# One-core attention with two expert layers: weights decoded by integer rounding, a third of the early decoding kept, and attention's order and engines from one table

## The chip, the cores and the metric

The kernel runs on one core of a Trainium2 chip. The metric is the device time of one execution in microseconds (us). Engines are named as in the profile: PE is the matrix engine and PEld its weight loads, DVE the vector engine, ACT the scalar engine, POOL the general engine, and SP the engine whose queue issues the DMA transfers.

## What is computed

Three steps follow one another, on 4 batches, 8 heads, 576 positions and 64 channels:

```python
scores = q @ k.T / sqrt(64);  scores[above diagonal] = -1e9
local  = softmax(scores) @ v
p      = where(q > 0, q + 1, exp(q))
mem    = (p @ M_prev) / (p @ z_prev + 1e-6)
x      = g * mem + (1 - g) * local            # g = sigmoid(beta), one per head
x      = x as [2304 tokens, 512]
x      = (silu(x @ w_gate) * (x @ w_val)) @ w_out        # inner width 1536
h      = x @ w_in                                        # inner width 2048
x      = where(h >= 1, h, where(h <= -1, 0, (h + 1)**2 / 4)) @ w_out2
```

All five weight arrays arrive as 64-bit floats, and the kernel itself turns them into 32-bit ones.

## The kernel before

**Numbers and products.** A 64-bit weight is two 32-bit words. `number` (L874 to L943) makes a 32-bit float of them: ACT takes the upper word without its sign (L892), DVE clamps it (L897), shifts it by the exponent's difference (L900) and puts the sign back (L903); a power of two cut from the result, times the lower word, is then added (L922). `split` (L953, L955) cuts a number into two rounded parts, hi and lo, and every product of the expert layers is a sum of three matmuls, hi by hi, lo by hi and hi by lo. The same is done with x: L831 and L834 in attention, `halves` (L1298 hi on ACT, L1301 lo on DVE) in the expert layers, which are called the MLP below.

**Attention** (0 to 254.8 us) goes over 16 pairs of heads. L644 and L678 make the scores, L658 masks them and takes the row maximum, L665 the exponential, L733 scales the rows (POOL; the last pair on DVE), L747, L749, L770 and L787 transpose, and L812 (`MZ`, the memory, times `P`) with L819 (values times `R`) make `av`, with the two heads in the two column halves of PE. `MZ` is padded with zeros to 128 rows. x goes to DRAM (`xs`, L848), already split. A planner (`Plan`) simulates the engines and puts the tasks of attention in order by a table of priorities (`ORDER`, `EARLY`, `COPY`) and each task has a fixed engine. A change of a matmul's form costs in it, and tasks of one form are kept together (`STAY`).

**Early work.** In attention's gaps POOL, DVE and ACT decode the first six of twelve blocks of `w_gate` and `w_val` (a block is 128 of the inner 1536 columns), and PE multiplies them with the x that is already there: L1170, 144 matmuls of 512 columns and 48 of 256. The results are put aside (`gv`, L1180).

**The MLP** has 2304 tokens in 6 groups of 384, two to a pair of groups. A second plan orders it by due times counted back from the end (`late_starts`):

- 254.8 to 366.4 us: `plain` (L1357), the rest of the first six blocks, 12 matmuls for one block and group;
- 366.4 to 496.4 us: `chain` (L1406), blocks 6 to 11, two blocks by two groups at a time in seven products instead of eight (`sums` and `x_pieces`, L1314 and L1335, form the sums of x that these need, `Weights.pair` those of the weights);
- 496.4 to 647.8 us: `down` (L1484), times `w_out`; 647.8 to 821.5: `w_in` in chains (L1406); 821.5 to 1018.5: `down2` (L1538).

x returns from `xs` by L1279, the early results by L1377, and the inner values are stored by L1368 and loaded again in `down`. SP issues all of these in the order of the plan; a load that waits holds up those behind it.

Of the kernel before, what the change touches and what calls it, by code (L numbers as in the profile page):

```python
# [11 lines left out]
U32 = mybir.dt.uint32  # L12
AF = mybir.ActivationFunctionType
# [5 lines left out]
P = 128  # L19
# [7 lines left out]
D0 = 6  # L27

FIRST_PAIRS = 3
STAY, TURN = 1.0e9, 165  # L30
# [3 lines left out]
EARLY = (-31758.7233, 79570.0368, -56626.7479, 43732.2004, 50493.6538, -22848.8291, 79748.7834, -38414.5005, 72019.3742, 35464.8591, 50747.3145, 30443.7461)  # L34
XH, GVO = 4, 3
X1, XS = 8, 25
RAW, WA, WH, TP, SU = 3, 5, 2, 7, 4
GROUP_AT, X_AT = (-58356.8242, -57686.563, -55609.5288), (21938.2824, -38157.4904, 79878.1715)
# [5 lines left out]
GV = (768, 512, 512)  # L44
# [1639 lines left out]
```

## Time and profile before

| what | us |
| --- | --- |
| median of three runs (1022.22 to 1025.65) | 1022.69 |
| the profiled execution | 1024.29 |
| its span | 1022.5 |
| PE busy in it | 1005.3 (98%) |
| DVE busy | 711.5 (70%) |
| ACT busy | 577.8 (57%) |
| POOL busy, all of it in attention | 214.5 (21%) |

The profiled execution has 1.8 us around its span and lies 1.6 us above the median. PE's shares are near the full span, so what counts is how much matmul work there is, in each stage, and where PE waits. The mean granted clock was 0.997.

### The profile page before, as it was taken

The numbers are of one execution on the slowest core, as the hardware profiler recorded it, in microseconds if no ns is written. First come the engines' busy times: TensorE is split into PE (matmuls) and PEld (weight loads), VectorE is DVE, ScalarE is ACT, GpSimd is POOL, SyncE is SP. The second block draws the span as 40 slices with busy tenths as digits, with TensorE's granted clock in tenths as the row PEclk, the third lists the DMA queues.
The fourth block names the chain that finished last, engine by engine and source line by source line (L and its number), as shares of the span: only waits on it lengthen the run. The fifth ranks groups of instructions, "written<-read, shape, count | busy, mean of one in ns | idle before, by whom it ended". The sixth has DMA issues, their size and how long they took to land.

```text
span 1022.5 us, 16609 instructions
## 1 busy us (share of the span) xinstructions
PE 1005.3 (98%) x5892; PEld 908.2 (89%) x5892; DVE 711.5 (70%) x1490; ACT 577.8 (57%) x1249; POOL 214.5 (21%) x300
## 2 busy tenths in 40 slices
PE   6999999999999999999999999999999999999998
PEld 5677777777999999999999999999999988888886
DVE  4887888885588777788778788876765346455451
ACT  5887898875333364636254444555444557567560
POOL 7899889893000000000000000000000000000000
PEclk8999999999999999999999999999999999999999
DMA  7787654327983542343976556255444596324420
GB/s 167 176 209 215 165 166 140 113 72 240 349 302 119 185 160 98 140 155 122 386 309 232 201 176 211 88 183 212 157 150 150 204 377 225 120 77 145 133 99 31
DMA packets 144547, 183.03 MB, mean 179 GB/s; under 512 B 70288, under 2 KB 101520, under 8 KB 144464
## 3 DMA queue, kind: packets, MB, share of 16 engines
q1 hardware_dynamic: 142366, 178.52, 52.9%
q0 software_dynamic: 768, 3.15, 0.9%
q8 instruction: 47, 0.77, 0.3%
q10 hardware_dynamic: 1330, 0.30, 0.1%
q14 instruction: 36, 0.29, 0.1%
HBM read 116.40 MB, written 65.54 MB: 178 GB/s over the span
## 4 chain that ended last, share of the span: by engine, by line
PE 93%; DMA 2%; POOL 2%; ACT 1%; DVE 1%; issue 0%; SPq 0%; ACTq 0%; DVEq 0%; POOLq 0%
PE mm L1406 30%; PE mm L1538 19%; PE mm L1484 13%; PE mm L1357 11%; PE av L819 4%; PE mm L1170 4%; PE s L644 3%; PE t L770 2%; PE av L812 2%; PE s L678 1%; POOL a L733 1%; DMA hs<-h 1%; PE t L787 1%; DMA xw<-park 1%; PE tp L598 1%; PE tq L540 1%
## 5 line engine op out<-in xcount | busy, mean ns | idle before, releaser
L1406 PE MATMUL mm<-xw 128*128 128x384 f32 x1512 | 269.5, 334 | 0.0
L1406 PEld LDWEIGHTS mm<-xw 128*128 128x128 f32 x1512 | 262.8, 188 | 0.1
L1538 PE MATMUL mm<-xw 128*128 128x512 f32 x864 | 196.2, 390 | 0.0
L1538 PEld LDWEIGHTS mm<-xw 128*128 128x128 f32 x864 | 162.2, 188 | 33.6
L1484 PE MATMUL mm<-xw 128*128 128x384 f32 x864 | 150.4, 335 | 0.3 <-DMA xw<-park 0.3
L1484 PEld LDWEIGHTS mm<-xw 128*128 128x128 f32 x864 | 149.8, 188 | 0.7 <-DMA xw<-park 0.7
L1357 PE MATMUL mm<-xw 128*128 128x384 f32 (+1 forms) x672 | 111.6, 327 | 0.0
L1357 PEld LDWEIGHTS mm<-xw 128*128 128x128 f32 x672 | 111.3, 188 | 0.2 <-DVE x L834 0.2
L733 POOL TENSOR_SCALAR a<-a,r,OGP 128x256 f32<-128x256 f32 (+4 forms) x135 | 90.7, 683 | 5.2 <-ACT a L665 3.4
L665 ACT ACTIVATE a<-a,mn 128x256 f32<-128x256 f32 (+3 forms) x128 | 71.0, 565 | 9.7 <-DVE mn L658 9.5
L1527 DVE SCALAR_TENSOR_TENSOR t<-r,t 128x768 f32<-128x768 f32 x48 | 46.0, 958 | 38.1 <-ACT t L1526 36.6
L1301 DVE TENSOR_TENSOR xw<-t,xw 128x768 fp32r<-128x768 f32 x48 | 45.9, 957 | 36.9 <-ACT xw L1298 36.9
L1298 ACT CAST xw<-t 128x768 fp32r<-128x768 f32 x48 | 40.1, 835 | 40.6 <-DVE t L1527 40.6
L658 DVE CUSTOM_DVE_ANT_0 a<-s,mask 128x512 f32<-128x512 f32 (+3 forms) x128 | 55.1, 485 | 5.8 <-PE s L644 5.5
L1428 ACT COPY mm<-mm 128x384 f32<-128x384 f32 x42 | 19.4, 463 | 67.8 <-PE mm L1406 67.7
L892 ACT ACTIVATE wA<-raw 128x512 f32<-128x512 f32 x68 | 45.8, 675 | 16.7 <-DMA raw<-in_moe_w_out_dram 7.3
L819 PEld LDWEIGHTS av<-R,vn 128*64 128x64 f32 x448 | 32.2, 137 | 21.2
L1406 PE MATMUL mm<-xw,wh 128*128 128x384 f32 x252 | 50.5, 334 | 0.0
L1524 ACT ACTIVATE t<-r,half 128x768 f32<-128x768 f32 x48 | 44.9, 936 | 8.1 <-DMA r<-h2s 7.7
L903 DVE SCALAR_TENSOR_TENSOR wA<-raw,wA 128x512 uint32<-128x512 uint32 x68 | 48.6, 715 | 0.6
L819 PE MATMUL av<-R,vn 128*64 128x320 f32 (+4 forms) x448 | 48.7, 357 | 0.0
L897 DVE TENSOR_SCALAR wA<-wA 128x512 f32<-128x512 f32 x68 | 29.6, 436 | 25.5 <-ACT wA L892 24.1
(143 smaller groups left out, 1546.7 us busy)
## 6 DMA issues: line engine op xcount, KB each, us to landing
h2s<-r SPq DMA_DIRECT2D x48, 384.0 KB, 4.2
r<-h2s SPq DMA_DIRECT2D x48, 384.0 KB, 3.8
raw<-in_moe_w_out_dram SPq DMA_DIRECT2D x28, 512.0 KB, 5.5
park<-pk SPq DMA_DIRECT2D x28, 512.0 KB, 6.4
hs<-h SPq DMA_DIRECT2D x36, 384.0 KB, 2.6
h<-hs SPq DMA_DIRECT2D x36, 384.0 KB, 6.0
xw<-park SPq DMA_DIRECT2D x24, 512.0 KB, 8.1
xs<-x SPq DMA_DIRECT2D x16, 576.0 KB, 3.7
```

Source lines behind the costliest of these rows:

```text
L658: nc.vector.tensor_tensor_reduce(a, st[f"s{h}{tag}"][:, at_[c]:at_[c] + kl[c]], self.mask0[:, 512 - kl[c]:512], -0.125, 3.0e38, ALU.add, A ...
L665: nc.scalar.activation(a, a, AF.Exp, bias=mn[:, o:o + 1], scale=-1.0, accum_out=sm[:, o, 0:1])
L733: eng.tensor_scalar(a, a, st["mn"]["r"][:, o:o + 1], self.OGP[:, n, o:o + 1], op0=ALU.mult, op1=ALU.mult)
L819: nc.tensor.matmul(o[rg][halves[h], c0:c1], st["vn"][:, kc, h], r, start=False, stop=i == len(terms[rg]) - 1, tile_position=(0, h * 64), s ...
L892: nc.scalar.activation(f32(s["F"]), f32(words(s["raw"])[:, :, 1]), AF.Abs)
L903: nc.vector.scalar_tensor_tensor(s["F"], words(s["raw"])[:, :, 1], 0xC0000000, s["F"], op0=ALU.bitwise_and, op1=ALU.bitwise_or)
L1301: nc.vector.tensor_sub(s["x"][:, :, 1], t(), f32(s["x"][:, :, 0]))
L1357: nc.tensor.matmul(o[:, 0:n], u["k"](pw, kt), qs[kt // 2, c]["at"](px, kt % 2)[:, span], start=(kt == 0 and i == 0), stop=(kt == KT - 1 an ...
L1406: nc.tensor.matmul(o, S["k"](k, pw, j), x[k]["at"](px, j), start=begin and not (i or j), stop=j == 1 and i == 2, skip_group_check=True)
L1484: nc.tensor.matmul(o, u["k"](pw, m), h["at"](px, j), start=(i == 0 and j == 0 and n == 0), stop=(i == F1 // 2 - 1 and j == 1 and n == 2), ...
L1527: x1 = add_dve(2 * HB, lambda raw=raw, t=t: nc.vector.scalar_tensor_tensor(t["get"](), raw["get"](), 1.0, t["get"](), op0=ALU.max, op1=ALU ...
L1538: nc.tensor.matmul(o, h["at"](px, j)[:, m * P:(m + 1) * P], u["w"][:, pw], start=(i == 0 and j == 0 and n == 0), stop=(i == F2 // 2 - 1 an ...
```

## The change

- `number` no longer multiplies by a power of two. ACT turns the lower word, times 2**-29, into an int32 (`tail`), and an integer addition to the float's bits rounds it (`whole`), in place of `power`, `rest` and the float addition. In attention it is on POOL, in the MLP it is a DVE instruction over the 16-bit halves of the words (shown as ISA, 1024 elements for 512 words). `pair` decodes two blocks in one tile of 1024 columns.
- Of the early blocks two are decoded and used in attention (`D0`: gate and val of two blocks by `GE` = 3 groups, L1288: 144 matmuls of 384 columns); four more (`NUMBERS`) are only decoded, and their numbers parked in DRAM (L1126 fetches them). Four of the six early blocks thereby go through the chains, in pairs: 1260 chain matmuls of gate and val instead of 756, and 144 plain ones (L1452) instead of 672.
- `xs` holds x unsplit. Four groups' x (`GQ`) is split in attention, the other two at the start of the MLP from loads that L1389 issues; the sums of x are made from such loads, not from the two parts.
- `MZ` isn't padded: L877 multiplies 64 rows by 64 columns for each head, in two diagonal corners of PE.
- `RANK` gives each task of attention its priority, and `CHOICE` one of two engines (POOL or DVE for the scaling and for the minimum, ACT or DVE for copies). Forms aren't kept together any more.
- `down` takes the pairs of blocks in the order 1, 2, 3, 4, 0, 5, fetches the early results itself, and `w_out` is decoded by a gate of its own.

On PE, at the end of attention and the start of the MLP, the kernel before has the last pair's values (`av`; `R` and `vn` its factors, the numbers behind them single tiles), all plain matmuls and then the chains:

```order
L812 MATMUL av_3761<-P,MZ_248 64x256 x2
L819 MATMUL av_3761<-R_3705,vn_234 64x256
L819 MATMUL av_3761<-R_3723,vn_234 64x256
L819 MATMUL av_3761<-R_3705,vn_234 64x128
L819 MATMUL av_3761<-R_3723,vn_234 64x128
L1357 MATMUL mm<-xw 128x256 x96
L1357 MATMUL mm<-xw 128x384 x576
L1406 MATMUL mm<-xw 128x384 x24
```

and the kernel after:

```order
L877 MATMUL av_3582<-P,MZ_236 64x256 x2
L884 MATMUL av_3582<-R_3539,vn_223 64x256
L884 MATMUL av_3582<-R_3577,vn_223 64x256
L884 MATMUL av_3582<-R_3539,vn_223 64x128
L884 MATMUL av_3582<-R_3577,vn_223 64x128
L1452 MATMUL mm<-xw 128x384 x144
L1501 MATMUL mm<-xw 128x384 x24
```

The plain matmuls between attention and the first chain are 144 now, 48 for each of groups 3, 4 and 5.

On SP's queue at the same place, the kernel before issues the last two transfers of x to `xs` with the early results (`gv`) between them, and the loads of split x (`xw<-xs`) behind them:

```order
L848 DMA xs_67<-x_3780 128x2x576
L1377 DMA h_3868<-gv0_0_68 128x2x384
L848 DMA xs_67<-x_3786 128x2x576
L1377 DMA v_3872<-gv0_1_69 128x2x384
L1377 DMA h_3874<-gv1_0_70 128x2x128
L1377 DMA v_3876<-gv1_1_71 128x2x128
L1377 DMA h_3880<-gv2_0_72 128x2x128
L1377 DMA v_3882<-gv2_1_73 128x2x128
```

and the kernel after has a load of the unsplit x (`xr<-xs`) between the last two transfers, five more behind them, and then the parked numbers:

```order
L910 DMA xs_67<-x_3488 128x576
L910 DMA xs_67<-x_3601 128x576
L1389 DMA xr_3693<-xs_67 128x2x384
L910 DMA xs_67<-x_3605 128x576
L1389 DMA xr_3695<-xs_67 128x2x384
L1389 DMA xr_3712<-xs_67 128x2x384
L1389 DMA xr_3714<-xs_67 128x2x384
L1389 DMA xr_3716<-xs_67 128x2x384
L1389 DMA xr_3731<-xs_67 128x2x384
L1126 DMA wp_3734<-num47_252 128x512
L1126 DMA wp_3734<-num57_253 128x512
```

The first and the second `xr` are the two halves of group 4's x; they need the second-to-last and the last pair's transfer.

The diff, cut to its core:

```diff
-D0 = 6
-FIRST_PAIRS = 3
-STAY, TURN = 1.0e9, 165
+TURN = 165
 AB, RB1, RB0 = 3, 2, 2
 WARM = 8
 CUTS = (0, 2, 4)
-XH, GVO = 4, 3
-X1, XS = 8, 25
-RAW, WA, WH, TP, SU = 3, 5, 2, 7, 4
+GVO, XR = 3, 1
+X1, XS = 11, 25
+RAW, WA, WH, TP, SU, RW, WP = 2, 1, 2, 7, 4, 1, 1
 NK = 3
 NG = 2 * NK
 HB = NT // NG
 HS = S // 2
 HT = 512
-GV = (768, 512, 512)
+D0, GE, GQ = 2, 3, 4
+NUMBERS = ((1, 0), (1, 1))
+DOWN = (1, 2, 3, 4, 0, 5)
...
-ORDER = {
-    "load": -32204.7671, "load_v": -35530.0543, "load_z": -43110.5018, "load_M": -20880.4184, "tk":
...
+CHOICE = (
+    "0001010000111101010001001011110101101101000000001000000100000110101010101000000100000101000010110000"
...
+RANK = (
+    67, 95, 302, 311, 404, 410, 436, 442, 520, 599, 473, 499, 596, 610, 637, 644, 653, 713, 719, 738, 445, 466,
...
+        if self.rank:
+            prio = self.rank[len(self.tasks)]
...
+    def choose(self, prio, options, deps=(), uses=()):
+        c = int(self.choice[self.chosen]) if self.chosen < len(self.choice) else 0
+        self.chosen += 1
+        eng, dur, fn, port = options[c]
+        t = self.add(eng, dur, prio, fn, deps, uses, port=port)
+        t["options"] = [x[:2] + x[3:] for x in options]
+        return t
...
-            eng = COPY[name]
-            def f():
+            def f(copy):
                 for src, dst, _ in parts:
-                    (nc.scalar.copy if eng == "ACT" else nc.vector.tensor_copy)(dst(), src())
-            cost = {"ACT": c_act, "DVE": c_dve2}[eng]
-            return add(eng, sum(cost(c) for *_, c in parts), name + ".cp", f, deps, uses)
+                    copy(dst(), src())
+            both = [("ACT", sum(c_act(c) for *_, c in parts), lambda: f(nc.scalar.copy), False),
+                    ("DVE", sum(c_dve2(c) for *_, c in parts), lambda: f(nc.vector.tensor_copy), False)]
+            return choose(name + ".cp", both, deps, uses)
...
-            eng = nc.vector if num == B * NP - 1 else nc.gpsimd
-            return add(*(("DVE", c_dve(cols)) if num == B * NP - 1 else ("POOL", c_pool(cols))), name + ".sc", f, [t_r],
-                       [i_a[key], i_mn])
+            both = [("POOL", c_pool(cols), lambda: f(nc.gpsimd), False),
+                    ("DVE", c_dve(cols) + 50, lambda: f(nc.vector), True)]
+            return choose(name + ".sc", both, [t_r], [i_a[key], i_mn])
...
-                        nc.tensor.matmul(o[rg][halves[h], 0:w], MZ()[:, h], st["P"][:, q0:q0 + w], start=True,
-                                         stop=False, tile_position=(0, h * 64), skip_group_check=True)
+                        nc.tensor.matmul(o[rg][halves[h], 0:w], MZ()[halves[h]], st["P"][halves[h], q0:q0 + w], start=True,
+                                         stop=False, tile_position=(h * 64, h * 64), skip_group_check=True)
...
-                def hi(name=name, q0=q0, w=w):
-                    nc.scalar.copy(mk_x()[:, 0, q0:q0 + w], st[name][:, 0:w])
-                def lo(name=name, q0=q0, w=w):
-                    nc.vector.tensor_sub(
-                        mk_x()[:, 1, q0:q0 + w], st[name][:, 0:w], f32(mk_x()[:, 0, q0:q0 + w]))
-                t = add("ACT", c_act(w), name + ".hi", hi, [t_av], [i_o[rg], i_x])
-                out.append(add("DVE", c_dve2(w), name + ".lo", lo, [t], [i_o[rg], i_x]))
+                def raw(copy, name=name, q0=q0, w=w):
+                    copy(mk_x()[:, q0:q0 + w], st[name][:, 0:w])
...
-        def power():
-            s["S"] = self.p["wS"].tile([P, 512], U32, name="wS", tag="wS")
-            nc.vector.tensor_scalar(s["S"], s["F"], 0xFF800000, None, op0=ALU.bitwise_and)
-        def rest():
-            nc.vector.scalar_tensor_tensor(
-                f32(s["S"]), words(s["raw"])[:, :, 0], 2.0 ** -52, f32(s["S"]), op0=ALU.mult, op1=ALU.mult)
-        def rest_a(i_L):
-            s["L"] = self.p["wA"].tile([P, 512], F32, name="wL", tag=f"wA{i_L.slot}")
-            nc.scalar.activation(s["L"], words(s["raw"])[:, :, 0], AF.Copy, scale=2.0 ** -52)
-        def rest_b():
-            nc.gpsimd.tensor_mul(f32(s["S"]), s["L"], f32(s["S"]))
+        def tail():
+            s["L"] = (self.p["wA"].tile([P, 512], I32, name="wL", tag=f"wA{i_L.slot}") if self.pooled
+                      else i32(words(s["raw"])[:, :, 0]))
+            nc.scalar.activation(s["L"], words(s["raw"])[:, :, 0], AF.Copy, scale=2.0 ** -29)
         def whole(eng):
-            eng.tensor_add(f32(s["F"]), f32(s["F"]), f32(s["S"]))
+            eng.tensor_add(i32(s["F"]), i32(s["F"]), s["L"])
...
+            t2 = None
             for on, took, fn, uses in (
                     (eng, cost, size, [i_raw, i_F]), ("DVE", e_dve(512), clamp, [i_F]),
-                    ("DVE", e_dve(512), shift, [i_F]), ("DVE", e_dve2(512), sign, [i_raw, i_F]),
-                    ("DVE", e_dve(512), power, [i_F, i_S]), ("DVE", e_dve2(512), rest, [i_raw, i_S]),
-                    ("DVE", e_dve2(512), lambda: whole(nc.vector), [i_F, i_S])):
+                    ("DVE", e_dve(512), shift, [i_F]), ("DVE", e_dve2(512), sign, [i_raw, i_F])):
                 t = plan.add(on, took, prio, fn, [t], uses)
-            return t
-        t = plan.add("ACT", c_act(512) + 40, prio, size, [t], [i_raw, i_F])
+                t2 = t2 or plan.add("ACT", e_act(512), prio, tail, [t], [i_raw])
+            return plan.add("DVE", e_dve2(512) + 130, prio, lambda: whole(nc.vector), [t, t2], [i_F, i_raw])
...
+    def numbers_early(self, plan, src, prio):
+        i_F, s = plan.inst("wA"), {}
+        t = self.number(plan, src, prio, s, i_F, [])
+        home = self.dram.tile([P, 512], F32, name=f"num{t['n']}")
+        plan.dma(prio, [728], lambda: self.nc.sync.dma_start(home, f32(s["F"])), [t], [i_F])
+        return home
...
+        steps = (
+                ("ACT", e_act(n), size, [i_raw, i_W]), ("DVE", e_dve(n), clamp, [i_W]), ("DVE", e_dve(n), shift, [i_W]),
+                ("ACT", e_act(n), tail, [i_raw, i_W]),
+                ("DVE", e_dve2(n), sign, [i_raw, i_W]), ("DVE", e_dve2(n), whole, [i_W]),
+                ("DVE", e_dve2(256), two(add, 4, 2, 3), [i_W]), ("DVE", e_dve2(256), two(sub, 2, 0, 2), [i_W]),
+                ("DVE", e_dve2(256), two(sub, 5, 4, 0), [i_W]), ("DVE", e_dve2(256), two(sub, 6, 1, 5), [i_W]))
+        for k, (on, took, fn, uses) in enumerate(steps):
+            if homes and k < 6:
+                continue
+            t = [plan.add(on, took, None, fn, t, uses)]
+            made[k] = t[0]
+        ends = [self.split(plan, None, [made[d]], lambda a=a, b=b: f32(W(a, b)), lambda j=j, m=(b - a) * 256: dst(j)[:, :, 0:m],
+                           (b - a) * 256, [i_W, places[j]], behind=free)
+                for j, (d, a, b) in enumerate(((7, 0, 3), (8, 3, 6), (9, 6, 7)))]
...
+                t = plan.dma(None, [1095], load, deps[r], [i_r], last)
+                t = wts.first(plan, None, hi, [t], [i_r], 2 * HB)
+                x["t"] = plan.add("DVE", c_dve2(2 * HB), None, lo, [t], [i_r], port=True)
...
+    def raw_x(kb, r, c, deps=()):
+        s = flat("xr")
+        s["d"] = plan.dma(None, [2.85 * HB], lambda: nc.sync.dma_start(s["get"](), xs[:, 2 * r:2 * r + 2, cols(2 * kb + c)]),
+                          deps, [s["i"]])
...
-    def x_pieces(qs, after=(), free=None):
-        r, made = {}, {}
-        for key in ((0, 0), (0, 1), (1, 1), (1, 0)):
-            r[key] = flat("xr")
-            def whole(key=key):
-                x = f32(qs[key]["x"])
-                nc.vector.tensor_add(r[key]["get"](), x[:, :, 0], x[:, :, 1])
-            made[key] = add_dve(2 * HB, whole, [qs[key]["t"], *after], [qs[key]["i"], r[key]["i"]])
-        t = lambda *ks: [made[x] for x in ks]
-        got = sums(r[0, 0], r[0, 1], r[1, 0], r[1, 1], (t((0, 0), (0, 1)), t((1, 1)), t(), t((1, 0))), free)
+    def x_pieces(kb, qs, free=None):
+        r = {key: raw_x(kb, *key, [xp[kb - 1][6]["t"]] if kb else []) for key in ((0, 0), (0, 1), (1, 1), (1, 0))}
+        t = {key: [r[key]["d"]] for key in r}
+        got = sums(r[0, 0], r[0, 1], r[1, 0], r[1, 1], (t[0, 0] + t[0, 1], t[1, 1], [], t[1, 0]), free)
         return {0: qs[0, 0], 1: qs[1, 0], 2: qs[1, 1], **got}
...
-        for i in range(F1 // 2):
+        for n, i in enumerate(DOWN):
             t = flat("h")
-            x = plan.dma(None, [2.85 * HB], lambda t=t, i=i: nc.sync.dma_start(t["get"](), hs[i][g]), [t_hs[i, g]],
-                         [t["i"]], behind=gate(H_AHEAD))
+            if i == 0 and g < GE:
+                x = from_gv(g, t)
+            else:
+                x = plan.dma(None, [2.85 * HB], lambda t=t, i=i: nc.sync.dma_start(t["get"](), hs[i][g]), [t_hs[i, g]],
+                             [t["i"]], behind=gate(H_AHEAD))
...
+    for g in range(GQ, NG):
+        for r in range(2):
+            x = raw_x(g // 2, r, g % 2)
+            qs[g // 2][r, g % 2] = halves(x["get"], x["i"], [x["d"]])
+    make(*todo[0])
+    xp[0] = x_pieces(0, qs[0])
     for i in range(D0 // 2):
-        for kb in (1, 2):
-            for c in range(2):
-                t = flat("h")
-                ends = [plain(f, qs[kb], c, slice(0, HB), t, []) for f in (2 * i, 2 * i + 1)]
-                t_hs[i, 2 * kb + c] = store(t, hs[i][2 * kb + c], ends)
-            if i == 1 and kb == 1:
-                xp[1] = x_pieces(qs[1], [xp[0][3]["t"]], seq[-1:])
-            if i == 2 and kb == 1:
-                make(*todo[0])
-        t = flat("h")
-        t_hs[i, 0] = store(t, hs[i][0], [from_gv(i, HB, 0, t, 4000)])
+        for g in range(GE, NG):
+            t = flat("h")
+            ends = [plain(f, qs[g // 2], g % 2, slice(0, HB), t, []) for f in (2 * i, 2 * i + 1)]
+            t_hs[i, g] = store(t, hs[i][g], ends)
+            if g == GQ - 1:
+                xp[1] = x_pieces(1, qs[1])
+    xp[2] = x_pieces(2, qs[2], seq[-1:])
     make(*todo[1])
-    xp[2] = x_pieces(qs[2], [xp[1][3]["t"]], seq[-1:])
+    down_f = [2 * i + c for i in DOWN for c in range(2)]
+    parks = [wts.parked(plan, out_rows(moe_w_out, f), gate(PARK_AHEAD)) for f in down_f]
```

## Rows read from the trace of the kernel before

**Rows 1.** Windows: us; busy (count) of PE, PEld, DVE, ACT, POOL; clock, DMA, GB/s

```profile
34.00:242.70 208.70, 205.39 (x1504) 152.25 (x1504) 173.08 (x551) 173.14 (x544) 189.86 (x236) 1.00 0.57 158
0.00:254.80 254.80, 241.93 (x1729) 179.24 (x1729) 195.99 (x620) 198.66 (x618) 214.55 (x300) 0.99 0.60 166
254.80:366.40 111.60, 111.60 (x674) 111.60 (x675) 82.91 (x140) 38.82 (x69) 0.00 (x0) 1.00 0.69 241
366.40:496.40 130.00, 130.00 (x752) 130.00 (x752) 107.05 (x216) 67.58 (x140) 0.00 (x0) 1.00 0.42 146
```

**Rows 2.** Chain that ended last, in order of time: start, us, engine, tile, line, count

```profile
90.82 6.97 PE mm L1170 x30
...
254.78 111.61 PE mm L1357 x672
366.38 130.00 PE mm L1406 x750
```

**Rows 3.** Groups of instructions by shape, PE: busy us, mean ns, idle before

```profile
L1357 PE MATMUL mm<-xw 128*128 128x384 f32 x576 | 100.0, 334 | 0.0
...
L1170 PE MATMUL mm<-xh,xw 128*128 128x256 f32 x48 | 6.0, 285 | 0.0
```

**Rows 4.** PE's timeline around two pairs' products: start, us, line, tiles, count

```profile
105.41 0.60 PE L747 MATMUL t<-ident,a 128*128 128x128 f32 x4
105.84 0.27 PE L749 MATMUL t<-ident,a 128*128 128x128 f32 x1
106.05 0.76 PE L812 MATMUL av<-P,MZ 128*64 128x320 f32 x4
106.64 2.23 PE L819 MATMUL av<-R,vn 128*64 128x320 f32 x20
108.69 0.60 PE L812 MATMUL av<-P,MZ 128*64 128x256 f32 x4
109.12 0.82 PE L819 MATMUL av<-R,vn 128*64 128x256 f32 x8
109.78 0.71 PE L812 MATMUL av<-P,MZ 128*64 128x320 f32 x4
...
112.80 0.82 PE L819 MATMUL av<-R,vn 128*64 128x256 f32 x8
113.55 0.73 PE L1170 MATMUL mm<-xh,xw 128*128 128x512 f32 x2
```

**Rows 5.** What PE waited for in attention: us in total, times, longest

```profile
PE t L770 <- POOL a L733: 5.2, 3, 3.9
PE t L770 <- DVE a L733: 1.8, 1, 1.8
```

**Rows 6.** DMA issues by tile: count, KB each, median us to landing

```profile
h<-hs SPq DMA_DIRECT2D x36, 384.0 KB, 6.0
...
r<-h2s SPq DMA_DIRECT2D x48, 384.0 KB, 3.8
...
xs<-x SPq DMA_DIRECT2D x16, 576.0 KB, 3.7
```

**Rows 7.** SP's timeline at attention's end

```profile
255.68 0.38 SPq L848 DMA_DIRECT2D xs<-x  x1
```

**Rows 8.** Groups by shape, DVE and ACT

```profile
L658 DVE CUSTOM_DVE_ANT_0 a<-s,mask 128x512 f32<-128x512 f32 x32 | 21.6, 686 | 4.2 <-PE s L644 4.2
...
L1365 DVE TENSOR_TENSOR h<-h,mm 128x384 f32<-128x384 f32 x24 | 13.3, 553 | 12.9 <-PE mm L1357 6.6 <-ACT xw L1298 3.0 <-issue 1.7
...
L1301 DVE TENSOR_TENSOR xw<-xr,xw 128x768 fp32r<-128x768 f32 x12 | 11.2, 952 | 0.0
...
L1298 ACT CAST xw<-xr 128x768 fp32r<-128x768 f32 x12 | 9.6, 833 | 2.1 <-DVE xr L1314 2.1
L658 DVE CUSTOM_DVE_ANT_0 a<-s,mask 128x128 f32<-128x128 f32 x32 | 9.1, 284 | 0.0
...
L1055 DVE TENSOR_TENSOR wC<-wA,wC 128x256 f32<-128x256 f32 x14 | 5.9, 418 | 0.0
```

More of the change, by code (lines that the diff above doesn't have):

```diff
@@ L104, with __init__ @@
     RELEASE = 90
-    def __init__(self, start=None, over=None, lat=None, slow=None, stay=0, turn=0, keep=False):
+    def __init__(self, start=None, over=None, lat=None, slow=None, stay=0, turn=0, keep=False, choice="", rank=()):
         self.slow, self.stay, self.turn, self.keep = slow or {}, stay, turn, keep
@@ L506, in pair @@
         else:
-            for t in pl.tasks[-2:]:
-                t["prio"] = (-1.0e6, t["n"])
-            first = pl.add("ACT", 4800, -1.0e6, load(*q_load, nc.scalar, self.gates()), uses=[i_q])
-            l_q = pl.add("DMA", 300, -1.0e6, lambda: None, [first], [i_q])
+            first = pl.add("ACT", 4800, None, load(*q_load, nc.scalar, self.gates()), uses=[i_q])
+            l_q = pl.add("DMA", 300, None, lambda: None, [first], [i_q])
         l_v = dma("load_v", [728, 728, 182], load(
@@ L1024, in whole, with pair, load, begin @@
         return s
-    def pair(self, plan, srcs, behind, free):
+    def pair(self, plan, srcs, behind, free, homes=None):
         nc = self.nc
-        i_F = [plan.inst("wA") for _ in srcs]
-        i_C = [plan.inst("wA") for _ in range(2)]
+        i_raw, i_W = None if homes else plan.inst("rw"), plan.inst("wp")
         places = [plan.inst("X"), plan.inst("X"), plan.inst("wh")]
-        s = [{}, {}]
-        w = {}
+        s, w = {}, {}
+        n = 2 * 512
+        def load(j):
+            if j == 0:
+                s["raw"] = self.p["rw"].tile([P, 2 * n], U32, name="rw", tag=f"rw{i_raw.slot}")
+            dst = s["raw"][:, j * n:(j + 1) * n].rearrange("p (k c) -> p k c", k=srcs[j].shape[1])
+            nc.sync.dma_start(dst, srcs[j])
+        word = lambda j: s["raw"].rearrange("p (n t) -> p n t", t=2)[:, :, j]
+        W = lambda a, b: s["W"][:, a * 256:b * 256]
+        F = lambda: W(0, 4)
+        S = lambda: W(4, 8)
+        def begin():
+            s["W"] = self.p["wp"].tile([P, 8 * 256], U32, name="wp", tag=f"wp{i_W.slot}")
+        def load_F(j):
+            if j == 0:
+                begin()
+            nc.sync.dma_start(f32(W(2 * j, 2 * j + 2)), homes[j])
+        def size():
+            begin()
+            nc.scalar.activation(f32(F()), f32(word(1)), AF.Abs)
+        def clamp():
+            nc.vector.tensor_scalar(f32(F()), f32(F()), LOW64, TOP64, op0=ALU.max, op1=ALU.min)
+        def shift():
+            nc.vector.tensor_scalar(F(), F(), 5, 2, op0=ALU.logical_shift_left, op1=ALU.logical_shift_right)
+        def sign():
+            nc.vector.scalar_tensor_tensor(F(), word(1), 0xC0000000, F(), op0=ALU.bitwise_and, op1=ALU.bitwise_or)
+        def tail():
+            nc.scalar.activation(i32(S()), word(0), AF.Copy, scale=2.0 ** -29)
+        def whole():
+            nc.vector.tensor_add(i32(F()), i32(F()), i32(S()))
+        def two(fn, o, x, y):
+            return lambda: fn(f32(W(o, o + 1)), f32(W(x, x + 1)), f32(W(y, y + 1)))
         def dst(j):
@@ L1066, in pair @@
-        at_ = ((0, 0), (0, 256), (2, 0), (0, 512), (1, 0), (1, 256), (1, 512))
-        need = (0, 0, 4, 2, 1, 1, 3)
-        return {"t": [ends[need[k]] for k in range(7)], "i": [places[at_[k][0]] for k in range(7)],
+        t = []
+        for j in range(2):
+            t.append(plan.dma(None, [728 if homes else 1456], lambda j=j: (load_F if homes else load)(j),
+                              uses=[i_W if homes else i_raw],
+                              behind=[s["load"]] if j else behind))
+            s["load"] = plan.last
```

345 lines of the change are left out of this document (155 added, 190 removed), and 92 rows, old and new, of tables (FIRST_ORDER, ORDER, RANK).

## The prediction

> **What bounds the kernel now.** I read the windows by stage first, then the chain of waits, then PE's groups and PE's waits in attention. The windows [rows 1] say that the MLP is PE alone: from 254.8 us PE is busy all of the time (111.60 of 111.60, 130.00 of 130.00), while DVE has 82.91 and 107.05 there. So a matmul less is time less, and DVE's or ACT's work costs nothing as long as it is in time. In attention PE is busy 241.93 of 254.80 us, and in its middle 205.39 of 208.70, although POOL is busy 189.86 there. PE bounds this stage too, with 3.3 us of gaps in the middle and 9.6 at its two ends. The chain agrees: it goes through the early products, the plain products and the chains without a pause between them [rows 2]. PE's waits in attention [rows 5] are few: 5.2 us on POOL's and 1.8 us on DVE's scaling of the rows (L733).
>
> **The change part by part.** All differences are against the profiled execution (1024.29 us, its span 1022.5).
>
> *Early products.* Thirty matmuls of 512 columns in a row take 6.97 us in the chain [rows 2], 0.232 each; 144 make 33.5 us. The 48 of 256 columns take 6.0 [rows 3]. Both go. In their place come 144 of 384 columns; 576 such took 100.0 us [rows 3], 0.1736 each, so 25.0. PE has 14.5 us less in attention: **-14.5**. This is a gain on the path because PE has almost no gaps in the middle; what fills in for it if another engine is late is rival B.
>
> *Plain products and chains.* The plain stage of 111.6 us goes [rows 2]; 144 matmuls remain, 25.0 us. The chains get 1260 - 756 = 504 more. 750 of them took 130.00 us [rows 2], 0.1733 each, so 87.4. Together -111.6 + 25.0 + 87.4 = **+0.8**. Seven products for eight save an eighth of four blocks' work, but the early work that is no longer done in attention eats it here.
>
> *Tiles of another form.* I counted how often the shape of PE's tile changes from one matmul to the next in the order of attention: 96 times before and 142 after. The increase is the corner tiles: L877 (64 rows by 64 columns) and L884 (128 by 64) alternate, 49 changes where L812 and L819 had one shape. What a change costs: transposes follow each other every 0.11 us (four from 105.41 to 105.84), but from the last, L749, to L812 it is 0.21; eight L819 take 0.66 before L812 (109.12 to 109.78) and 0.75 before L1170 (112.80 to 113.55) [rows 4]. So 0.09 to 0.10 a change, and 46 x 0.09 = **+4.1**, bounds 0 and 4.6. The Trainium skill says in "TensorEngine Tiling (Array Packing)", section Key Properties, that a change of the tiling mode, not of the tile alone, drains TensorE. The trace agrees, with 0.09 us beside it; if a corner and a column half counted as one mode under that rule, this term would be 0.
>
> *Attention's order and engines.* The tables let DVE, POOL and ACT share scaling, minimum and copies. Of PE's waits on L733 [rows 5] between none and all go, -7.0 to 0, and as many new ones as PE's middle has gaps now may come, +3.3. Nearest is the single wait on DVE of 1.8, of the last pair, which is the sort a freer choice removes: **-1.8**. DVE gets more: 673 instructions instead of 620 by the order, at the present mean of 195.99 / 620 = 0.316 us [rows 1] that is 212.7 us in some 242, 88%. POOL has 91% in the middle now while PE runs on, so 88% need not bind.
>
> *Start of the MLP.* After the change 48 plain matmuls of group 3 (8.3 us) are all the work that needs no fresh x. Group 4 needs both its halves; the second half's load stands in SP's queue behind the last pair's transfer and waits for its landing. Call the end of attention T (254.8). The last transfer was issued at 255.68 [rows 7], T + 0.9, and lands in 3.7 [rows 6], T + 4.6. The load takes between 3.8 and 6.0 (the two loads of 384 KB in [rows 6]), then 0.83 on ACT and 0.95 on DVE for hi and lo [rows 8]: ready between T + 10.2 and T + 12.4. Six of group 4's matmuls can run on its first half, so it is needed at T + 9.4. The stall is 0.8 to 3.0. Behind the waiting load stand the four other loads of x and the parked numbers, all of them for later chains; DVE waits for them. Then DVE has to keep up: up to the third set of x sums it has 32 operations of 768 columns (0.952), 10 of 384 (0.553), 8 of 256 (0.418) [rows 8] and three on 512 (some 1.6), 41.0 us in all, while PE has 25.0 + 3 x 42 x 0.1733 = 46.8. In the chains before DVE was busy 107.05 of 130.00, 82% [rows 1]; at that share 41.0 us take 49.8, 3.0 more than there is. Sum 0 to 6.0; I take the middle of both, 1.9 and 1.5: **+3.4**.
>
> *Decoding.* For 512 numbers DVE loses a cut, a product and an addition and gets one integer addition over 1024 halves; ACT gets one pass. Its price isn't in the trace: from L658, 0.686 for 512 columns and 0.284 for 128 [rows 8], a column costs 1.047 ns, so 1024 would be 1.22 us, and as cheap as a plain addition of 512 would be 0.686. Either is less than what goes, and DVE in the MLP has spare time outside the stretch above: **0**. If the cover were gone in the whole chain stage, a saving couldn't show either, since PE is full. The same holds for the parked numbers' transfers, for half as large transfers to `xs`, and for the later order in `down`.
>
> **Sum:** -14.5 + 0.8 + 4.1 - 1.8 + 3.4 = **-8.0 us**, so 1016.3 for a profiled execution. The profiled one lies 1.6 us above the median of the runs, so I predict 1014.7 for that median. With all low ends it is -14.5 + 0.8 - 7.0 = -20.7 (1002), with all high ends -14.5 + 0.8 + 4.6 + 3.3 + 6.0 = +0.2 (1023).
>
> **Rivals.**
>
> *A, slower: the two corners run one after the other.* Before, two heads' L812 lie beside each other: a stretch of both takes 0.59 (106.05 to 106.64) for 320 columns and 0.43 (108.69 to 109.12) for 256 [rows 4]. If the 64 by 64 tiles of L877 couldn't overlap, each pair of heads would take 1.02 us more, 16 pairs 16.3, and the kernel 1014.7 + 16.3 = 1031. It decides from two thirds of that loss on (11.1 us, 1025.8). For it: both corners write the same tile `av`. Against it: the two column halves do that now and overlap. The Trainium skill, same page, section Restrictions and Gotchas, "Gotcha 1: PSUM Pressure", says that different row tiles cannot access the same PSUM bank at once, which speaks for this rival; no row of before has two row tiles at work together, so the trace neither agrees nor contradicts. Chance 0.14.
>
> *B, no gain: DVE becomes attention's bound.* 212.7 us of DVE less the 22.9 it has outside the middle (195.99 - 173.08, [rows 1]) leave 189.8 in the middle. At POOL's 91% that needs 208.6 us, just what the middle lasts now: the 14.5 us that PE gains turn into waits for DVE, the mode changes lie in them, and the MLP's +0.8 remains: 1023.5. For it: DVE's instructions are in a chain (mask, scale, copy) that PE waits on in every pair. Against it: POOL's load falls by a third of its instructions (300 to 192), so that DVE's waits for its data get shorter, and the share of 88% is below what POOL stands now. Chance 0.17.
>
> *C, a larger gain.* All waits on L733 go (-7.0) and the start of the MLP has no stall: -14.5 + 0.8 + 4.1 - 7.0 = -16.6, 1006. For it: the scaling can go to the engine that is free. Against it: the new tasks for DVE, and T + 9.4 before the earliest T + 10.2. Chance 0.14.
>
> **How the numbers follow.** The forecast has the remaining 0.55, and by itself a range of 1010 to 1020. 0.3% is 3.1 us, about what a measurement of this kernel can tell from no change: faster is below 1019.6, slower above 1025.8. Faster: 0.51 of the forecast, 0.14 of C and 0.02 of B, 0.67. Same: 0.03, 0.12 of B and 0.01 of A, 0.16. Slower: 0.13 of A, 0.03 of B and 0.01 of the forecast, 0.17. The range 1003 to 1028 holds the forecast, most of B and C, and leaves out most of A and a rest of C, some 0.16.
>
> **What would show it.** In the profile after: attention's end at about 242 to 246 us by the first plain matmul; a gap of 1 to 3 us on PE after 48 plain matmuls, with L1404 or a load of `xr` as the releaser; plain products and first chains of some 25 + 218 us; everything behind them as long as before. The first L877 of a pair lasting 0.4 to 0.6 us speaks for the term of the forms, 0.9 or more for A. PE's waits on DVE in attention adding up to more than 10 us speak for B. I am wrong in the main step if attention is shorter by under 5 us with PE still full, for then the early matmuls weren't worth what the chain shows.

## The result and the profile after

The changed kernel takes 1011.38 us (median of 4 runs, 1010.75 to 1012.60) against 1023.47 for the kernel before; the ratio is 0.9881, 95% interval 0.9860 to 0.9902. The forecast was 1014.7 in a range of 1003 to 1028: the sign and the range hold, the gain is half as large again as the forecast one. The profiled execution takes 1011.54 us, its span 1009.7, 12.8 less than before where the sum said 8.0.

The windows of the profile after, by the same stages as [rows 1] (us; busy and count of PE, PEld, DVE, ACT, POOL; clock, DMA share, GB/s):

```profile
34.00:230.00 196.00, 195.67 (x1468) 142.61 (x1467) 169.41 (x588) 171.85 (x527) 102.36 (x128) 1.00 0.49 131
0.00:239.70 239.70, 229.42 (x1680) 166.02 (x1680) 195.55 (x672) 195.42 (x592) 124.37 (x187) 0.99 0.51 133
239.70:264.80 25.10, 25.10 (x147) 25.08 (x146) 16.30 (x25) 13.66 (x21) 0.00 (x0) 1.00 0.76 257
264.80:483.90 219.10, 218.03 (x1256) 217.39 (x1256) 169.31 (x291) 131.38 (x239) 0.00 (x0) 1.00 0.50 172
```

The first plain matmul starts at 239.72 instead of 254.78, so attention is 15.1 us shorter (forecast 14.5 - 4.1 + 1.8 = 12.2), and what follows is 2.3 us longer, 770.0 instead of 767.7 (forecast 4.2). POOL has lost 90 us of work in attention, DVE and ACT have as much as before. PE's waits, to be read beside [rows 5]:

```profile
PE tk L589 <- DMA kn<-in_k_dram: 5.6, 1, 5.6
PE s L743 <- issue: 1.3, 1, 1.3
PE s L743 <- POOL e L642: 1.2, 1, 1.2
PE idle L1242 <- DVE still L1236: 1.0, 1, 1.0
PE mm L1501 <- DVE xw L1404: 1.0, 1, 1.0
```

No wait on the scaling of rows is left (L798, formerly L733: 5.2 and 1.8), and the first chains wait once, 1.0. But most of the 5.2 stood at the very start, 3.91 before 18.93 us and 0.82 before 20.95, and there the kernel after waits 5.57 for the first `kn`:

```profile
18.93 0.66 PE L770 MATMUL t<-ident,a 128*128 128x128 f32 x4 [3.91 <-POOL a L733]
...
10.39 1.09 PE L589 MATMUL tk<-ident,kn 128*128 128x128 f32 x4 [5.57 <-DMA kn<-in_k_dram]
```

In the first 34 us PE is idle 9.5 us before and 9.9 after. It is the middle that has become tight: 208.70 - 205.39 = 3.3 us of gaps before, 0.3 after (196.00 and 195.67 above). PE's timeline at the last two pairs shows the products of a pair, to be read beside [rows 4]:

```profile
231.18 0.76 PE L877 MATMUL av<-P,MZ 64*64 64x320 f32 x4
231.87 2.28 PE L884 MATMUL av<-R,vn 128*64 128x320 f32 x20
234.07 0.65 PE L877 MATMUL av<-P,MZ 64*64 64x256 f32 x4
234.65 0.87 PE L884 MATMUL av<-R,vn 128*64 128x256 f32 x8
235.45 0.76 PE L877 MATMUL av<-P,MZ 64*64 64x320 f32 x4
...
239.72 20.55 PE L1452 MATMUL mm<-xw 128*128 128x384 f32 x117
```

From one pair's first product to the next pair's it takes 4.27 us (231.18 to 235.45); before it was 3.73 (106.05 to 109.78 in [rows 4]).

To see where attention's 15.1 us come from I added up, over PE's whole timeline of attention, the time from each entry's start to the next one's, less the idle time listed with it. Short waits that aren't listed stay with their line:

| PE in attention, us | before | after | difference |
| --- | --- | --- | --- |
| early products (L1170; L1288) | 42.1 | 27.2 | -14.9 |
| products with `MZ` and values (L812, L819; L877, L884) | 61.0 | 68.5 | +7.5 |
| transposes of the rows (L747, L749, L770, L787; L812, L814, L835, L852) | 48.5 | 45.8 | -2.7 |
| scores (L644, L678; L709, L743) | 59.0 | 57.4 | -1.6 |
| the rest of its work | 31.6 | 30.7 | -0.9 |
| listed idle | 11.6 | 9.0 | -2.6 |

The first row is the forecast's term to 0.4 us. The second is nearly double its +4.1. The last four are 7.8 together. The transposes and scores are the same instructions in the same number in both kernels, so I take their differences for waits too short to be listed; that is argued from the sums, and no run shows it by itself. The forecast had 1.8 for all of this.

### The profile page after: what moved, and what is told of

Read it like the earlier page. It is cut to its first block, busy times and chain, and to the rows that moved or that the text cites. A ratio compares the mean times of both kernels' runs of the same rounds, so it can differ in the third digit from the quotient of the medians.

```text
span 1009.7 us, 16216 instructions
## 1 busy us (share of the span) xinstructions
PE 994.7 (99%) x5820; PEld 895.8 (89%) x5820; DVE 676.5 (67%) x1396; ACT 628.3 (62%) x1278; POOL 124.4 (12%) x187
## 4 chain that ended last, share of the span: by engine, by line
PE 91%; DMA 4%; DVE 2%; SPq 1%; ACT 1%; issue 1%; POOL 0%; ACTq 0%; DVEq 0%; POOLq 0%
PE mm L1501 38%; PE mm L1636 19%; PE mm L1582 15%; PE av L884 4%; PE s L709 3%; PE mm L1288 3%; PE t L835 2%; PE av L877 2%; DMA qn<-in_q_dram 1%; PE s L743 1%; DMA xr<-xs 1%; PE t L852 1%; PE t L812 1%; DMA wp<-num 1%; PE tp L658 1%; SPq L523 1%
## 5 line engine op out<-in xcount | busy, mean ns | idle before, releaser
L1501 PE MATMUL mm<-xw 128*128 128x384 f32 x1944 | 347.3, 334 | 1.1 <-DVE xw L1404 1.0
L1501 PEld LDWEIGHTS mm<-xw 128*128 128x128 f32 x1944 | 337.6, 188 | 2.5 <-DVE xw L1404 1.3
L1636 PEld LDWEIGHTS mm<-xw 128*128 128x128 f32 x864 | 162.1, 188 | 33.6
L1582 PE MATMUL mm<-xw 128*128 128x384 f32 x864 | 150.1, 334 | 0.0
L1582 PEld LDWEIGHTS mm<-xw 128*128 128x128 f32 x864 | 149.8, 188 | 0.0
L1501 PE MATMUL mm<-xw,wh 128*128 128x384 f32 x324 | 64.8, 334 | 0.0
L798 POOL TENSOR_SCALAR a<-a,r,OGP 128x512 f32<-128x512 f32 (+4 forms) x81 | 58.8, 737 | 42.9 <-PE tp L658 11.7
L723 DVE CUSTOM_DVE_ANT_0 a<-s,mask 128x256 f32<-128x256 f32 (+3 forms) x128 | 56.3, 484 | 11.3 <-PE s L709 11.3
L1523 ACT COPY mm<-mm 128x384 f32<-128x384 f32 x54 | 25.1, 465 | 54.3 <-PE mm L1501 53.9
L1501 PEld LDWEIGHTS mm<-xw,wh 128*128 128x128 f32 x324 | 56.9, 188 | 0.0
L884 PEld LDWEIGHTS av<-R,vn 128*64 128x64 f32 x448 | 29.8, 136 | 28.7 <-issue 12.1
L884 PE MATMUL av<-R,vn 128*64 128x320 f32 (+4 forms) x448 | 50.6, 364 | 0.0
L508 ACT COPY R<-t 128x384 f32<-128x384 f32 (+3 forms) x133 | 47.8, 432 | 3.3 <-PE t L835 2.4
L1401 ACT CAST xw<-h 128x768 fp32r<-128x768 f32 x36 | 29.7, 834 | 27.2 <-DMA h<-hs 14.2
L1404 DVE TENSOR_TENSOR xw<-h,xw 128x768 fp32r<-128x768 f32 x36 | 34.0, 954 | 15.7 <-ACT xw L1401 15.7
L709 PE MATMUL s<-K,S 64*128 64x128 f32 (+3 forms) x256 | 42.1, 457 | 0.0
```

Source lines behind the costliest of these rows:

```text
L508: copy(dst(), src())
L709: nc.tensor.matmul(out[h][:, at_[c]:at_[c] + kl[c]], st["S"][halves[h], c * P:(c + 1) * P], st["K"][halves[h], 0:kl[c]], start=True, stop= ...
L723: nc.vector.tensor_tensor_reduce(a, st[f"s{h}{tag}"][:, at_[c]:at_[c] + kl[c]], self.mask0[:, 512 - kl[c]:512], -0.125, 3.0e38, ALU.add, A ...
L798: eng.tensor_scalar(a, a, st["mn"]["r"][:, o:o + 1], self.OGP[:, n, o:o + 1], op0=ALU.mult, op1=ALU.mult)
L884: nc.tensor.matmul(o[rg][halves[h], c0:c1], st["vn"][:, kc, h], r, start=False, stop=i == len(terms[rg]) - 1, tile_position=(0, h * 64), s ...
L1401: nc.scalar.copy(s["x"][:, :, 0], t())
```

## The experiments

Two theories stood against each other at first. One is the prediction's: PE alone bounds attention, so its work is the time. The rival is that the other engines' chain stands so close behind PE that a matmul less buys a wait. The price of the corner tiles was a question of its own.

**1. Padding back.** `MZ` is padded to 128 rows again, and the corners become column halves:

```diff
-MZ()[halves[h]], st["P"][halves[h], q0:q0 + w] ... tile_position=(h * 64, h * 64)
+MZ()[:, h], st["P"][:, q0:q0 + w] ... tile_position=(0, h * 64)
```

> The kernel after, with the memory matrix padded with zeros again (128 rows by 64 columns for each head, as in the kernel before), so that these matmuls have the same tile shape as the values' products behind them. Theory (changes of the tile's shape cost PE time on the path, 7.5 us in the products of the 16 pairs): 1011.4 - 7.5 = 1003.9, span of a pair of products 3.73 us again instead of 4.27. Rival (the time of these products is hidden, since another engine sets attention's end): 1010 to 1012.

1007.73, ratio 0.9847 (0.9832 to 0.9862), 3.6 below the kernel after. Attention ends at 234.08, 5.6 earlier, and the pair takes 3.78 us from `MZ` product to plain product:

```profile
230.30 0.71 PE L879 MATMUL av<-P,MZ 128*64 128x320 f32 x4
230.84 2.22 PE L886 MATMUL av<-R,vn 128*64 128x320 f32 x20
232.89 0.60 PE L879 MATMUL av<-P,MZ 128*64 128x256 f32 x4
233.33 0.82 PE L886 MATMUL av<-R,vn 128*64 128x256 f32 x8
234.08 2.20 PE L1454 MATMUL mm<-xw 128*128 128x384 f32 x11
```

Summed as above, the products fall by 6.9 and PE's listed idle time rises by about 2. Later, two chains of `w_in` wait 0.8 for a copy of ACT (L1529). So the corners' cost is on the path, but not all of it comes back.

**2. Grouping the corners.** All four corner products of a pair first, then all values:

```diff
+                for rg in range(2):
                     for i, (c0, c1, kc, at_) in enumerate(terms[rg]):
```

> The kernel after, with all four corner matmuls of a pair (both column ranges) in front of all its value products, so that the shape changes twice per pair of heads instead of four times. Theory (each change costs, some 0.12 us): half of 7.5 us come back, 1007.6. Rival (the corners themselves are slower, because the two only partly run side by side; a change costs nothing): 1011.4, with the same total for the corners and the values.

1006.96, ratio 0.9841 (0.9826 to 0.9855), 4.4 below the kernel after; this beats both kernels. Two changes of shape per pair are gone, 32 in all, and the products take 63.6 instead of 68.5. So the changes cost, about 0.15 us each here. By the run before it is 0.14: padding takes the changes of shape in PE's order of attention from 142 to 92, and 6.9 us for these 50 went. I had read 0.09.

**3. A third of each early product.** One matmul instead of three for each part of the sum in L1288:

```diff
-                        for n, (pw, px) in enumerate(PARTS):
-                            nc.tensor.matmul(..., u["k"](pw, kt), x[r]["at"](px, kt % 2), ...)
+                        nc.tensor.matmul(..., u["k"](0, kt), x[r]["at"](0, kt % 2), ...)
```

> The kernel after with one of the three parts of each early product only (hi by hi), so 48 early matmuls instead of 144; the early results lack the other two parts. Theory (PE bounds attention, an early matmul is worth what the chain shows): 96 x 0.1736 = 16.7 us less, 994.7. Rival (DVE, at 82% of attention, would become the bound at once): less than 5 us are gained, 1006 to 1011, and PE's waits on DVE or ACT grow by 12.

1003.32, ratio 0.9801 (0.9786 to 0.9815): 8.1 less. Attention ends at 230.77, 9.0 earlier, while the early products lost 15.5 by the sum above. Neither theory: a matmul less was worth a bit over half of itself. The rest went into idle time (+3.4) and into the transposes (+3.1). About 1.1 of the 3.1 is the clock. PE waited 1.25 and 0.91 for copies of ACT, and the granted clock, at 1.00 before, had a mean of 0.87 from 155 to 160 us and of 0.79 from 160 to 165, between its two levels (1.2 and 2.4 GHz). Seven transposes that take 0.93 elsewhere took 1.70:

```profile
146.94 0.93 PE L835 MATMUL t<-ident,a 128*128 128x128 f32 x7
...
159.05 1.01 PE L1287 MATMUL mm<-xw 128*128 128x384 f32 x2 [0.91 <-ACT R L508]
159.86 1.70 PE L835 MATMUL t<-ident,a 128*128 128x128 f32 x7
```

**4. No early products.** `GE` = 0; the tables skip the entries of these tasks.

> The kernel after with no early products at all: the first two blocks' 144 matmuls for groups 0 to 2 move from attention to the start of the MLP (288 plain matmuls there), the order of the rest of attention unchanged. Theory (an early matmul costs attention what a plain one costs the MLP): attention 27.3 us shorter by the chain, the MLP 25.0 longer, and the wait of 1.0 at the first chains gone: 1008, bounds 1006 to 1011. Rival (early products fill time in which PE would wait): attention only 14 us shorter, 1021 or more.

1037.49, ratio 1.0139 (1.0120 to 1.0158), 26 us slower than the kernel after. Attention ends at 240.37, as late as with the products, and PE's listed idle time goes from 9 to 25 us. The MLP is 25.0 longer, as forecast. The order did not stay, though: without these tasks the planner placed the others anew, and the rest of PE's sequence differs from that of the kernel after (in experiment 3 it is the same). So this run holds a change of order too. A wait and a fall of the clock behind it show in its timeline and windows:

```profile
215.38 1.58 PE L877 MATMUL av<-P,MZ 64*64 64x320 f32 x4 [3.29 <-DVE P L508]
216.88 4.32 PE L884 MATMUL av<-R,vn 128*64 128x320 f32 x20
```

```profile
200.00:215.00 15.00, 11.62 (x86) 7.37 (x86) 10.12 (x35) 9.81 (x32) 8.28 (x12) 0.98 0.14 41
215.00:225.00 10.00, 9.62 (x59) 5.89 (x60) 4.43 (x13) 3.31 (x11) 2.79 (x4) 0.69 0.08 30
```

PE was busy 11.62 of 15 us and waited 3.29 at their end; in the next 10 us the granted clock had a mean of 0.69 (0.50, the lower of its two levels, from 215 to 221), and the same twenty products took 4.32 us instead of 2.28. The rival's side holds, but attention did not even become the 14 us shorter that it had.

**5. The kernel before with fewer early matmuls.** Is attention of before like that too? Two of the three parts, nothing else:

```diff
-                        for n, (pw, px) in enumerate(PARTS):
+                        for n, (pw, px) in enumerate(PARTS[1:]):
```

> The kernel before with two of the three parts of each early product (hi by hi and hi by lo), so 128 early matmuls instead of 192, everything else in its order; the early results lack one part. It cuts PE's work in attention by (33.5 + 6.0) / 3 = 13.2 us, about what the change cuts (14.5), and leaves decoding, order and engines as they are. Theory of the prediction (PE alone bounds attention): attention ends 13.2 us earlier, 1010. Rival (the other engines' chain, POOL at 91% first, stands close behind PE, and the change was needed to relieve it): at most 7 us, 1016 or more, and PE's waits in attention grow by 6 or more.

1018.02, ratio 0.9944 (0.9930 to 0.9957): 5.8 less, attention 7.8 shorter (246.96). The early products lost 12.4 by the sum; the waits took back 4.3 listed, and the transposes 2. The rival holds: the cut alone gives 7.8 of its 12.4 in attention. PE's waits:

```profile
PE t L770 <- POOL a L733: 7.5, 9, 4.2
PE tm L534 <- DMA kn<-in_q_dram: 3.4, 3, 1.5
PE t L770 <- DVE a L733: 3.2, 1, 3.2
```

The 2 in the transposes are for the most part no wait but the clock behind one. The last pair's wait on DVE grew from 1.80 to 3.23; behind it the granted clock had a mean of 0.66 over 5 us, where it stays at 1.00 before, and the same eighteen transposes lasted until 237.01, 3.63 us, instead of 2.02 (to 244.81). The first two rows are from the kernel before:

```profile
242.79 2.19 PE L770 MATMUL t<-ident,a 128*128 128x128 f32 x18 [1.80 <-DVE a L733]
244.81 0.49 PE L787 MATMUL t<-ident,a 128*128 128x128 f32 x3
...
233.38 3.79 PE L770 MATMUL t<-ident,a 128*128 128x128 f32 x18 [3.23 <-DVE a L733]
237.01 0.49 PE L787 MATMUL t<-ident,a 128*128 128x128 f32 x3
...
233.00:238.00 5.00, 4.62 (x28) 4.62 (x29) 2.89 (x6) 0.94 (x2) 0.00 (x0) 0.66 0.96 325
```

**6. The first engine of every choice.** `choice=""` with the priorities as they are.

> The kernel after with the first engine of each choice (scaling, minimum and the second parts on POOL, copies on ACT), the priorities as they are. Theory (after the change DVE, ACT and POOL stand just behind PE, so that sharing the work between them counts): PE waits for ACT or POOL, attention 5 us longer or more, 1016 to 1035. Rival (the order counts, the engines don't): 1010 to 1013.

1036.81, ratio 1.0120 (1.0107 to 1.0134): 25 us slower, attention until 265.46. POOL is busy 206.24 us of the first 239.7 instead of 124.37, DVE 132.26 instead of 195.55. The planner, which reckons with the engines, also put PE's tasks in another order.

**7. Rounding in the MLP alone**, in the kernel before:

```diff
-                    ("DVE", e_dve(512), power, ...), ("DVE", e_dve2(512), rest, ...), ("DVE", ..., whole ...)
+                t2 = t2 or plan.add("ACT", e_act(512), prio, tail, [t], [i_raw])
+            return plan.add("DVE", e_dve2(512) + 130, prio, rounded, [t, t2], [i_F, i_raw])
```

> The kernel before with the integer rounding in the MLP only: three DVE passes of 512 (cut, product, addition) replaced by one integer addition on DVE and one pass on ACT, for each of the 56 blocks; attention decodes as before. Theory (DVE's work in the MLP is covered by PE): no change, 1022 to 1025, with DVE some 40 us less busy. Rival (a share of PE's work in the MLP waits for decoding): 2 us or more less.

1023.97, ratio 1.0001 (0.9992 to 1.0010). DVE has 463.82 us of work from 254.8 us on instead of 515.50, and the time doesn't move. As forecast: decoding is covered in the MLP.

**8. The grouped kernel once more.**

> The kernel after with the corner matmuls grouped, as in the run before, once more for its trace beside the next.

One run of 1006.39; attention ends at 234.11, in experiment 2 at 234.63. Its use is as a second trace for experiment 12.

**9 and 10. Less decoding in attention of before**, with two parts of the early products and with all three:

```diff
-        t = plan.add("DVE", c_dve(512), prio, power, [t], [i_F, i_S], port=True)
+        t = plan.add("DVE", c_dve(512), prio, lambda: None, [t], [i_F, i_S], port=True)
```

and the same for `rest_a`, `rest_b` and `whole`.

> The kernel before with two of three parts of each early product, as in the run of two parts, and in attention without the lower words: for the 12 early blocks the cut on DVE (0.467 us each), the pass on ACT (0.692) and the product and the addition on POOL (1.280 and 1.344) are left out, so the weights of these blocks lack their lower words. It takes 31.5 us from POOL, 5.6 from DVE and 8.3 from ACT; the order stays. Theory (POOL's load is what kept the two-part kernel from gaining its 13.2 us): 3 us or more below the 1018.0 of that run, 1010 to 1015. Rival (the order, or DVE and ACT, hold it): 1017 to 1019.

> The kernel before without the lower words of the early blocks, as in the run before, with all parts of the early products. Theory (PE is the bound while it has this much work, and waits only 5.2 us on POOL): 2 to 5 us less, 1019 to 1022. Rival (POOL alone sets attention's end in the kernel before): 8 us less or more, 1016 or below.

1015.31, ratio 0.9925 (0.9910 to 0.9939), for the first; 1022.35, ratio 0.9993 (0.9980 to 1.0006), for the second. Without the cut on PE the relief buys nothing that stands clear of the noise; with it, 1.9 us by the ratios, between what the two theories said. In the first, POOL is busy 157.78 us in 34 to 230 (185.66 in experiment 5), and still PE waits at nearly the same places:

```profile
PE t L770 <- POOL a L733: 5.8, 4, 3.9
PE t L770 <- DVE a L733: 3.3, 1, 3.3
```

Two single waits of 3.9 and 3.3 are most of that. The 3.9 ends at 18.74 us, before POOL's share in 34 to 230 could bear on it, and the kernel before has the same wait; the 3.3 is that of the last pair, for DVE. PE's waits on POOL's scaling after 34 us did shrink, from 3.4 in experiment 5 to 1.3. So what the relief could reach it took, and that was little.

That the second run gained nothing is again in part the clock. Its last pair's transposes start at 240.69 instead of 242.79, but the granted clock had a mean of 0.54 from 241 to 244, and of the 2.1 us only 0.5 were left at the end of attention (254.32):

```profile
240.69 3.60 PE L770 MATMUL t<-ident,a 128*128 128x128 f32 x18 [1.90 <-DVE a L733]
```

**11. All scaling on POOL**, in the kernel after:

```diff
-            return choose(name + ".sc", both, [t_r], [i_a[key], i_mn])
+            pl.chosen += 1
+            return add(*both[0][:2], name + ".sc", both[0][2], [t_r], [i_a[key], i_mn])
```

> The kernel after with all the scaling of rows on POOL (144 instead of 81 instructions there), every other choice of the table as it is. Theory (it is the sharing of the scaling that keeps POOL from stopping PE): more than half of the 25 us that the run with the first choice everywhere lost, 1024 or more, with PE waiting on L798. Rival (the copies on DVE instead of ACT carry it): 1011 to 1015.

1036.12, ratio 1.0123 (1.0102 to 1.0144): all of what experiment 6 lost. POOL is busy only 132.16 of 196 us in the middle, so not by its share; PE waits for single scalings that come late, and after the longest of these waits, 6.26 to 51.96, the granted clock had a mean of 0.78 from 52 to 60. Here too PE's order is another:

```profile
PE t L813 <- POOL a L798: 9.3, 2, 6.3
```

**12. The stores of the plain stage on POOL's queue**, on the grouped kernel:

```diff
-            t_hs[i, g] = store(t, hs[i][g], ends)
+            t_hs[i, g] = store(t, hs[i][g], ends, nc.gpsimd)
```

> The kernel after with the grouped corners, and with the three stores of the plain stage issued by POOL's queue, which is idle then, instead of SP's, where two of them held up the loads of x behind them for 9.3 us. Theory (the wait at the first chains comes from these loads): about 1 us below the 1007.0 of the grouped kernel, 1005.5 to 1006.3. Rival (DVE is full there and sets it): 1006.6 to 1007.4.

1008.94, ratio 0.9862 (0.9848 to 0.9877), above the grouped kernel by 2 us, though the two intervals overlap. The wait at the first chains is there as before:

```profile
277.02 4.43 PE L1502 MATMUL mm<-xw 128*128 128x384 f32 x24 [1.00 <-DVE xw L1405]
```

This does not clear the loads. They were held up all the same, by another wait: the loads and the stored tiles take the same buffers (`flat`), and SP now stood before three loads of x until stores had landed. What SP waited for between 235 and 275 us:

```profile
SPq L1390 <- DMA hs<-h: 15.7, 3, 7.8
```

So whether late loads or DVE's own load make the wait is open. DVE is busy 18.92 of the 20 us around it (258 to 278), with one pause of 0.79, for a load of x; no run took its work away or gave the loads buffers of their own. The 2 us are in attention, which ends at 236.23 although all engines have the same order there; PE's listed waits in it are 12.0 instead of 8.9, and why is open.

## Why the prediction was right, and where not

- **What bounds the kernel.** That the MLP is PE alone holds: experiment 7 takes 51.7 us from DVE there and nothing changes, experiment 4 adds 144 matmuls and 25.0 us. That PE alone bounds attention was wrong. A full PE in the windows said only that PE had enough to do while the others worked. The other chain stood close behind: taking 12.4 and 15.5 us from PE in an unchanged order (experiments 5 and 3) shortened attention by 7.8 and 9.0, and taking 27 in another order (experiment 4) by -0.6. What was lost are waits and, behind the longer of them, some microseconds at a lower clock, which the prediction did not think of.
- **Early products, -14.5.** The amount is right (14.9), the step "a gain on the path because PE has almost no gaps" failed. Alone in the kernel before a cut of this kind gives somewhat over half in attention. That it came through whole here, since the waits went at the same time, is how the sums add up; no run makes this cut with the new order alone.
- **Order and engines, -1.8.** The term that was sized wrong most: listed and hidden waits fell by 7.8. The forecast took one wait on L733 of 1.8, where all 7.0 went, while the wait for the first inputs grew from 1.62 to 5.57, and didn't see that PE's other work would become shorter too. Experiments 6 and 11 show that with these priorities the table's sharing of the scaling is needed (25 us), 9 that a lighter POOL isn't enough. Order and choice weren't separated: the priorities came with these engines, and the same priorities with others are a third order.
- **Tiles of another form, +4.1.** Right in mechanism, nearly half too small: +7.5 in the products. The 46 changes were counted rightly, but each costs 0.14 to 0.15 us, not 0.09 (experiments 1 and 2). By the Trainium skill's rule ("TensorEngine Tiling (Array Packing)", Key Properties), that a changed mode drains the engine, the direction was to be had; the price is from experiments 1 and 2.
- **Start of the MLP, +3.4.** Too large: 2.3 - 0.8 = 1.5. No stall came after group 3's 48 matmuls (all 144 took 25.1), so the first half of the term was 0. With T now 239.72, the load of group 4's second half went out at T + 2.8 (242.54), where the sum had T + 4.6 from a row of transfers of 576 KB; the transfer in front of it has 288 now. Its lo part was ready at T + 8.3, before the T + 9.4 at which it was needed. One wait of 1.0 at the first chains is what is left of the second.
- **Decoding, 0.** Right by experiment 7; the integer addition took its low bound (below).
- **Rival A** fell: the two heads' corner products of 320 columns (four records) take 0.69 us with their change of shape; one after the other they would take 1.18. Both corners write one tile `av` and still lie side by side. What the Trainium skill says in "Gotcha 1: PSUM Pressure" (same page), that different row tiles cannot access one PSUM bank at once, cost no such time here. The prediction's "no row of before has two row tiles at work together" overlooked the scores: L644 already multiplies two heads in two row halves (64 by 128), and its records start in pairs 6 to 8 ns apart. Each head has a PSUM tile of its own there (`places`), so that row spoke against rival A, though not on the one tile `av`.
- **Rival B** as priced did not come: DVE stands at 195.55 of 239.7 us, 82%, since 672 instructions average 0.291 us and not 0.316. Its idea, that PE's gain turns into waits, is in part what experiments 3 and 5 show. **Rival C** was right that all waits on L733 go, and had the corners as much too small as the forecast.
- That the number came so near is in part luck, since the errors partly cancel: -0.4 on the early products, -6.0 on waits, +3.4 on the corners, -1.9 on the MLP's start are -4.9 together, against the -4.8 by which the profiled execution lies below its forecast.

## What to carry to other kernels

A stage whose main engine is 98% busy isn't thereby bound by it alone: before counting a matmul less as time less, take some away (or look at how the operand's producers stand behind), since the next chain may be close: here 12.4 of attention's 254.8 us taken from PE gave 7.8. Look for lost time also in the lines that have no listed gap, by comparing the time per instruction, and look at the granted clock of the stretch before calling it a wait. Before an edit to an order is called one change, compare the orders in the traces; a planner may have moved the rest. Count the changes of tile shape on PE; four corner products in a row instead of two and two gave 4 us here for a moved loop.

## What the hardware showed

The integer addition on DVE over 1024 16-bit halves (listed as CUSTOM_DVE_ANT_0) takes 0.688 us, as long as the float addition of 512 words that it replaces (L922, 0.686, the prediction's low bound). The integer addition of 512 words on POOL takes twice that. In attention four of the eight are on POOL, the other four on DVE:

```profile
L922 DVE TENSOR_TENSOR wA<-wA,wS 128x512 f32<-128x512 f32 x56 | 38.4, 686 | 0.5
...
L978 DVE CUSTOM_DVE_ANT_0 wA<-raw,wA 128x1024 uint16<-128x1024 uint16 x28 | 19.3, 688 | 1.5
...
L978 POOL TENSOR_TENSOR wA<-wA,wL 128x512 int32<-128x512 int32 x4 | 5.8, 1448 | 19.1 <-DVE wA L969 19.1
```

A wait on PE can cost more than its own length. In experiment 5 the last pair's wait of 3.23 us was followed by 5 us at a mean granted clock of 0.66, and the same eighteen transposes took 1.6 us longer; in experiment 4, with longer gaps, the mean was 0.69 over 10 us. In the kernel after, PE has 0.3 us of gaps between 34 and 230 us, and the clock stays at 1.00 there.
